# Attention, MLP and mixture of experts on one core: the experts' stage issued in source order, casts placed behind the copies of the products' banks, superblock border and last pair rearranged

## The chip, the cores and the metric

The kernel runs on 1 core of a Trainium2 chip. The metric is the device time of one execution in microseconds (us), smaller is better. Engines are called PE (matrix products), DVE (VectorE), ACT (ScalarE), POOL (GpSimd) and SP (the engine that issues DMAs here).

## The reference

```python
x = attention(q, k, v)                 # linear attention, 2304 tokens x 512
h = x @ moe_w_in; x = max(0.01 * h, h) @ moe_w_out          # 512 -> 2048 -> 512
P = exp(x @ w_gate - max)              # 2304 x 8
for _ in range(8):
    P /= P.sum(1, keepdims=True) + 1e-09; P /= P.sum(0, keepdims=True) + 1e-09; P *= N / E
for e in range(8):
    out += P[:, e:e + 1] * (np.maximum(x @ w1[e], 0.0) @ w2[e])   # 512 -> 1024 -> 512
```

All in fp32. The kernel splits each fp32 matrix into a high part (a cast on ACT) and a low part (a subtraction of that cast, mostly on DVE), and makes three products of them.

## The kernel before, in words

The first quarter computes attention and the MLP. What concerns the change is the experts' stage behind it. It treats the tokens in three superblocks of 768 (`NSB`) and the experts' hidden units in 32 pairs of 128-unit blocks (`NQ`), so there are 96 groups (`NG`), numbered `i`; groups 0 to 31 are superblock 0, 32 to 63 superblock 1, 64 to 95 superblock 2. Each `group(i)` is seven half steps, `t0` to `t6`. In `t0` to `t3` PE makes the seven products of a Strassen-like scheme, six matmuls each, in four PSUM banks (`pa` to `pd`): `pa`, `pb`, `pc`, `pd`, then `pa`, `pc`, `pd` a second time, accumulated on top. Between the two uses of a bank, ACT has to copy its first content out (`c1` from `pa`, the two halves of `c2` from `pc` and `pd`; lines 866, 881, 883). In `t4` to `t6` PE makes the second layer of the pair of groups before: in superblock 0 three token tiles of twelve 512-column matmuls (`y_tile`, tiles `e`), from group 34 on the seven products of `y_pass` (tiles `e` too, 384 columns).

Superblock 0 also prepares the experts' weights. `pair_load` and `second_load` bring the raw pair from DRAM to `mo_t`; POOL makes sums of its quarters (`pair_sums`, `second_sums`); `split` casts on ACT and subtracts on DVE (`pair_w1`, `pair_w2`, `second_split`); `keep` stores the split weights in DRAM (`d`). `second_split` uses three staging buffers in turn (`stage`). Superblocks 1 and 2 read the split weights back through a ring of buffers (`ring_load`). There DVE applies relu and the gate's weight (`relu_p`, into `mo_t`), POOL and DVE subtract (`sub_raw`), and `op_split` casts and subtracts the second layer's operands. In `y_pass`, ACT copies three of the products out (`snap`) and POOL adds them to `c22`; DVE adds the other four (`into`). At a border of superblocks `x_next` makes the split sums of the next 768 tokens. `y_out` transposes a superblock's result on PE, and stores it.

The first stage's order is written by hand (`tc.manual_schedule` for PE, ACT, POOL and SP). `front.close()` ends that before group 0, so in the experts' stage a scheduler orders every engine. The helper that issues all products has one line:

```python
    def split(hi, lo, a):
        nc.scalar.copy(hi, a)
        return lambda: nc.vector.tensor_tensor(lo, a, r32(hi), op=ALU.subtract)
```

The lambda is called in the next half step, by `drain`.

Of the kernel before, what the change touches and what calls it, by code (L numbers as in the profile page):

```python
# [22 lines left out]
def kernel(  # L23
# [163 lines left out]
    def bank(name):  # L187
        pool, tag = spare[0]
        spare.append(spare.pop(0))
        return pool.tile([P, 512], F32, tag=tag, name=name)  # L190

# [192 lines left out]
    def balance():  # L384
        nc.vector.tensor_reduce(mrow, lg, axis=AX.XY, op=ALU.max)
        yield PE_NEXT
        pt = bank("pmx")[:1, :P]
        nc.tensor.transpose(pt, mrow, ident)
        nc.vector.tensor_reduce(mall, pt, axis=AX.X, op=ALU.max, negate=True)
        yield PE_NEXT  # L390
        pt = bank("pmb")[:, :1]
        mm(pt, ones[:1, :], mall, True, True)
        nc.vector.tensor_copy(mneg, pt)
        yield
        nc.scalar.activation(pm, lg, AF.Exp, bias=mneg)
        yield
        for it in range(8):
# [6 lines left out]
            nc.vector.tensor_reduce(cs, pm.rearrange("p t e -> p e t"), axis=AX.X, op=ALU.add)  # L404
            yield PE_NEXT
            pt = bank(f"pcs{it}")[:, :E]
# [7 lines left out]
            yield  # L414
        ready.add("pm")
        yield
        for n, (r0, r1) in enumerate(((0, P), (P, TT * E))):
            yield PE_NEXT
            pt = bank(f"pT{n}")[: r1 - r0, :P]
# [92 lines left out]
    def split(hi, lo, a):  # L512
        nc.scalar.copy(hi, a)  # L513
        return lambda: nc.vector.tensor_tensor(lo, a, r32(hi), op=ALU.subtract)  # L514
# [10 lines left out]
    def pair_w1(i, part):  # L525
# [3 lines left out]
        return split(w1(i)[:, 0, 4:], w1(i)[:, 1, 4:], s_t())  # L529

# [29 lines left out]
    def second_sums(g):  # L560
        a11, a12, a21, a22 = second_quads(g)
        nc.gpsimd.tensor_tensor(a22, a21, a22, op=ALU.add)
        nc.gpsimd.tensor_tensor(a21, a11, a21, op=ALU.subtract)
        nc.gpsimd.tensor_tensor(a11, a22, a11, op=ALU.subtract)
        nc.gpsimd.tensor_tensor(a12, a11, a12, op=ALU.subtract)

    def second_split(g, k):
        a11, a12, a21, a22 = second_quads(g)
        name, a = (("S1", a22), ("S3", a21), ("S2", a11), ("S4", a12))[k]
# [3 lines left out]
        with tc.issue_after(mark[0].ins):  # L573
            f = split(v[:, 0], v[:, 1], a)
# [7 lines left out]
    def x_sums(sb):  # L582

        b = [
# [4 lines left out]
        b11, b12, b21, b22 = b  # L589
        if sb:  # L590
            t1 = hp_.tile([P, KC // 2, BLK], F32, tag="hh", name=f"t1_{sb}")
        else:
            t1 = mo(0, XS // 2).rearrange("p (c n) -> p c n", c=KC // 2)
# [4 lines left out]
        def both(name, a):  # L598
            split(xt(name)[:, 0], xt(name)[:, 1], a)()
            ready.add(("xt", sb, name))  # L600
# [14 lines left out]

    def x_next(sb):
        f = x_sums(sb)
        for i, n in ((0, 2), (2, 4), (4, 5), (6, 8), (5, 6), (8, 9), (9, 11)):
            for g in f[i:n]:
                g()  # L620
            if n in (2, 4, 5, 8):
                yield

    ring = []
    for i in range(NQ, NG + 2):
        if i < NG:
            ring += [d1[i % NQ][WA[n]] for n, _ in FIRST]
        g = i // 2 - 1
        if g >= NQ // 2:
            ring += [d2[g % (NQ // 2)][i % 2, WA[n]] for n, _, _ in SECOND]  # L630
# [26 lines left out]
    def product(o, i, an, bn, start=True):  # L657
# [4 lines left out]
        else:  # L662
            assert FIRST[used[0] % 7 if used[0] < 21 else (used[0] - 21) % 14 - 7][0] == an
# [30 lines left out]
    def relu_split(i, th, u, p):  # L694
        o = hid(i, th)[:, :, u]
        mark[0] = nc.scalar.activation(o[:, 0], p, AF.Relu)
# [37 lines left out]
    def y_pass(g, dt):  # L734
# [7 lines left out]
        bk = {}  # L742
# [10 lines left out]
        def into(a, b):  # L753
            if first_ and a is not c22:
                nc.scalar.copy(a, bk[b])
            else:
                nc.vector.tensor_tensor(a, bk[b], a, op=ALU.add)  # L757

        def step(n):
            an, bn, b = SECOND[n]  # L760
            assert ("op", g, bn) in ready, (g, bn)
            start = b not in bk
# [5 lines left out]
            if bn in ("B11", "T1", "T3"):  # L768
                snap(b)
            else:  # L770
                into({"B21": c11, "B22": dd, "T2": c22, "T4": cc}[bn], b)
            if last and n == 6:
                active.append([y_out(sb, dt, ya), None])

        return step

    def y_out(sb, dt, ya):
# [4 lines left out]
        for th, quads in enumerate(((c11, cc), (dd, c22))):  # L782
            for t in range(TB):
                if t % 2 == 0:
                    yield PE_NEXT
                tt = th * TB + t
                pt = bank(f"po{sb}_{dt}_{tt}")[:, : 2 * P]
# [15 lines left out]
    mark = [None]  # L803

    def group(i):
# [5 lines left out]
        nxt = i + 1 < NQ  # L811
# [6 lines left out]
        if g >= NQ // 2:  # L818
            step = y_pass(g, i % 2)
# [7 lines left out]
        def second_ops(t):  # L827
# [3 lines left out]
            if half == 0 and g >= 0:  # L831
# [5 lines left out]
                if t in (5, 6):  # L837
                    rest.append(second_split(g, t - 5))
            if half == 1:
                if t in (0, 1) and g >= 0:  # L840
                    rest.append(second_split(g, 2 + t))
                if t == 2 and i < NQ:
                    second_load(i - 1)
                    second_load(i)
                if t == 5 and i < NQ:
                    rest.append(pair_w2(i - 1))
                if t == 6 and i < NQ:
                    rest.append(lambda: keep_w2(i - 1))

        def t0():  # L850
            drain((late, rest))
            second_ops(0)
# [6 lines left out]
            if i >= NG:  # L859
                return  # L860
            if i < NQ:
                keep_w1(i)
            if nxt:
                pair_sums(i + 1)
# [3 lines left out]
            add(c1, bk[1], c1)  # L868

        def t1():  # L870
            drain()
            second_ops(1)
# [5 lines left out]
            if i >= NG:  # L878
                return
            product(bk[2], i, "S1", "T1")  # L880
            mark[0] = nc.scalar.copy(c2[:, 1], bk[2])
# [3 lines left out]
            add(c2[:, 1], c2[:, 1], c1)  # L885

        def t2():
            drain()
            second_ops(2)
            if i == NQ + 1:  # L890
                ring_load(18, 22)
            if i >= NG:
                return
# [7 lines left out]
            if i < NQ:  # L901
                pair_load(i + 2)

        def t3():
            if i >= NG:
# [246 lines left out]
```

## Time and profile before

| | us |
|---|---|
| median of 3 runs (lowest, highest) | 2041.34 (2037.67, 2042.96) |
| the profiled execution's own time | 2042.34 |
| its span, first to last instruction | 2040.6 |
| PE busy in the span | 1959.7 (96%) |
| DVE, ACT, POOL busy | 1521.5, 799.2, 678.3 |

The profiled execution stands 1.0 us over the median and 1.7 us over its own span. A busy PE can be a slow PE: its granted clock is a column of the stretches below.

### The profile page before, as it was taken

What the parts mean: (1) busy time and instruction counts of PE and PEld (TensorE: products, weight loads), DVE (VectorE), ACT (ScalarE), POOL (GpSimd) and SP (SyncE); (2) the same over time, 40 slices, a digit from 0 to 9 for tenths busy, and PEclk for the clock granted to TensorE, in tenths of its full rate; (3) what the DMA queues carried; (4) which work ended last, traced back from release to release, by engine and by line L of the source; (5) the groups of instructions that cost most, each with busy time, mean ns of one, the idle gap of its engine ahead of it and who ended that gap; (6) DMA issues with size and microseconds to landing.
All of it is one profiled execution on the core that took longest, in us unless ns stands there. A gap on an engine that the chain in (4) does not pass through costs nothing.

```text
span 2040.6 us, 30223 instructions
## 1 busy us (share of the span) xinstructions
PE 1959.7 (96%) x10757; PEld 1872.9 (92%) x10757; DVE 1521.5 (75%) x2193; ACT 799.2 (39%) x1481; POOL 678.3 (33%) x536
## 2 busy tenths in 40 slices
PE   7999999999998999999999999999989999999998
PEld 6999999999888888888889999999989999999997
DVE  7766535354886778776786888898897888888886
ACT  6744323243543444444333333333343333333332
POOL 4123313111243535343322333334332343343333
PEclk8999999999999999999999999999999999999999
DMA  6402201111678787878768878788777887778784
GB/s 238 165 11 73 62 21 52 42 57 68 216 270 309 257 309 252 307 256 307 259 214 299 252 234 267 254 254 255 253 224 234 257 257 253 253 234 268 252 248 145
DMA packets 237108, 430.44 MB, mean 211 GB/s; under 512 B 19984, under 2 KB 38560, under 8 KB 236960
## 3 DMA queue, kind: packets, MB, share of 16 engines
q1 hardware_dynamic: 236960, 428.51, 63.9%
q8 instruction: 87, 1.43, 0.3%
q14 instruction: 61, 0.50, 0.1%
HBM read 306.20 MB, written 122.23 MB: 210 GB/s over the span
## 4 chain that ended last, share of the span: by engine, by line
PE 40%; DVE 8%; ACT 2%; DMA 1%; issue 1%; POOL 1%; SPq 0%; POOLq 0%; ACTq 0%; DVEq 0%
PE e L193 22%; PE pa L193 5%; PE pc L193 5%; PE pd L193 5%; DVE xs L514 2%; PE pb L193 2%; DVE wa L514 2%; DVE acc L757 2%; DVE mo_t L730 1%; ACT xs L513 1%; DVE c L817 1%; POOL acc L751 1%; ACT c L866 0%; DMA mo_t<-in_w 0%; ACT wa L513 0%
## 5 line engine op out<-in xcount | busy, mean ns | idle before, releaser
L751 POOL TENSOR_TENSOR acc<-acc,acc 128x384 f32<-128x384 f32 x188 | 236.8, 1260 | 406.6 <-ACT acc L750 403.8
L193 PE MATMUL e<-xs,wb_t 128*128 128x384 f32 x1452 | 272.4, 335 | 0.0
L193 PE MATMUL e<-wb_t,xs 128*128 128x512 f32 x1152 | 272.2, 394 | 0.0
L193 PEld LDWEIGHTS e<-wb_t,xs 128*128 128x128 f32 x1152 | 218.4, 190 | 45.2 <-DVE xs L697 0.4
L513 ACT CAST wa<-mo_t 128x768 fp32r<-128x768 f32 (+2 forms) x189 | 159.0, 846 | 242.2 <-DVE mo_t L716 74.9
L193 PEld LDWEIGHTS e<-xs,wb_t 128*128 128x128 f32 x1452 | 253.4, 188 | 0.4
L193 PE MATMUL e<-wa,wb_t 128*128 128x384 f32 x1236 | 235.3, 335 | 5.8 <-DVE acc L757 5.5
L514 DVE TENSOR_TENSOR wa<-mo_t,wa 128x768 fp32r<-128x768 f32 (+2 forms) x189 | 209.9, 1121 | 30.9 <-ACT wa L513 30.5
L193 PEld LDWEIGHTS e<-wa,wb_t 128*128 128x128 f32 x1236 | 216.0, 188 | 7.3 <-DVE acc L757 6.5
L757 DVE TENSOR_TENSOR acc<-e,acc 128x384 f32<-128x384 f32 x244 | 124.1, 546 | 119.2 <-POOL acc L751 118.7
L513 ACT CAST xs<-mo_t 128x768 fp32r<-128x768 f32 x122 | 101.9, 836 | 233.7 <-DVE mo_t L716 93.3
L730 POOL TENSOR_TENSOR mo_t<-mo_t 128x768 f32<-128x768 f32 x64 | 118.5, 1852 | 218.8 <-DVE mo_t L716 211.8
L211 DVE TENSOR_TENSOR hh<-g,hh 128x384 fp32r<-128x384 f32 x96 | 60.5, 630 | 147.8 <-ACT g L210 147.6
L193 PE MATMUL pa<-xs,wb_t 128*128 128x384 f32 x744 | 154.1, 341 | 15.1 <-ACT c L866 13.6
L193 PEld LDWEIGHTS pa<-xs,wb_t 128*128 128x128 f32 x744 | 130.0, 188 | 23.8 <-ACT c L866 23.7
L514 DVE TENSOR_TENSOR xs<-mo_t,xs 128x768 fp32r<-128x768 f32 x122 | 141.6, 1177 | 13.3 <-ACT xs L513 13.3
L193 PE MATMUL pc<-xs,wb_t 128*128 128x384 f32 x744 | 150.7, 337 | 0.0
L193 PE MATMUL pd<-xs,wb_t 128*128 128x384 f32 x744 | 149.7, 335 | 0.0
L716 DVE SCALAR_TENSOR_TENSOR mo_t<-c,mo_t 128x768 f32<-128x768 f32 (+1 forms) x128 | 138.1, 1081 | 3.1
L209 ACT ACTIVATE hh<-ph 128x384 fp32r<-128x384 f32 x96 | 47.3, 493 | 233.1 <-PE y L193 218.3
L520 POOL TENSOR_TENSOR mo_t<-mo_t 128x256 f32<-128x256 f32 x32 | 28.5, 891 | 323.3 <-DMA mo_t<-in_w 190.3
L193 PEld LDWEIGHTS pc<-xs,wb_t 128*128 128x128 f32 x744 | 132.6, 190 | 0.0
(152 smaller groups left out, 3659.2 us busy)
## 6 DMA issues: line engine op xcount, KB each, us to landing
wb_t<-d SPq DMA_DIRECT2D x882, 256.0 KB, 3.2
d<-wa SPq DMA_DIRECT2D x32, 1792.0 KB, 9.1
d<-wb_t SPq DMA_DIRECT2D x90, 512.0 KB, 4.1
mo_t<-in_w SPq DMA_DIRECT2D x64, 512.0 KB, 6.2
raw<-in_wm SPq DMA_DIRECT2D x32, 512.0 KB, 3.7
d<-wa SPq DMA_DIRECT2D x22, 512.0 KB, 3.3
mo_t<-pd SPq DMA_DIRECT2D x32, 192.0 KB, 6.6
v<-in_vt SPq DMA_DIRECT2D x16, 320.0 KB, 5.6
```

The lines of the kernel that those rows point to most:

```text
L193: nc.tensor.matmul(o, a, b, start=start, stop=stop, **more)
L209: nc.scalar.activation(hh[:, 0, :], p, AF.Prelu, alpha=0.01)
L211: nc.vector.tensor_tensor(hh[:, 1, :], g, r32(hh[:, 0, :]), op=ALU.subtract)
L513: nc.scalar.copy(hi, a)
L514: return lambda: nc.vector.tensor_tensor(lo, a, r32(hi), op=ALU.subtract)
L520: nc.gpsimd.tensor_tensor(s[:, 0], a21, a22, op=ALU.add)
L716: nc.vector.scalar_tensor_tensor(o, p, 0.0, r, op0=ALU.max, op1=ALU.mult)
L730: eng.tensor_tensor(raw_q(o), raw_q(x), raw_q(y), op=ALU.subtract)
L751: nc.gpsimd.tensor_tensor(c22, c22, t, op=ALU.add)
L757: nc.vector.tensor_tensor(a, bk[b], a, op=ALU.add)
L817: add = lambda o, x, y: nc.vector.tensor_tensor(o, x, y, op=ALU.add)
```

## The change

Manual order now holds to the end of the program on PE, ACT, POOL and SP: `front.close()` moves behind the last group. DVE's order stays the scheduler's. Inside the groups, `second_ops` and several `op_split` are called behind the products and copies of their half step, and some in another half step; two of the four `second_sums` go from POOL to DVE; the loads of `second_load` go from `t2` to `t0` and `t1`; the casts of the second pair of groups are prepared in the first stage. At the border, sums of the next tokens (`x_ahead`) are made on POOL ahead of time. In `y_pass` the fourth bank is added to `c22` last. The passes of the last two pairs move by a group (`passes`), and the last pass subtracts straight from the banks and stores by column quarter (`y_last`).

```diff
-    def split(hi, lo, a):
+    def split(hi, lo, a, eng=nc.vector):
...
     def second_sums(g):
-        nc.gpsimd.tensor_tensor(a22, a21, a22, op=ALU.add)
+        nc.vector.tensor_tensor(a22, a21, a22, op=ALU.add)
         nc.gpsimd.tensor_tensor(a21, a11, a21, op=ALU.subtract)
-        nc.gpsimd.tensor_tensor(a11, a22, a11, op=ALU.subtract)
+        nc.vector.tensor_tensor(a11, a22, a11, op=ALU.subtract)
...
+    def x_split(sb, name, a):
+        eng = nc.gpsimd if sb > 1 and name in ("B11", "T2") else nc.vector
+        f = split(xt(name)[:, 0], xt(name)[:, 1], a, eng)
...
+    def x_ahead(sb):
...
+        nc.gpsimd.tensor_tensor(t1, b12, b11, op=ALU.subtract)
+        nc.gpsimd.tensor_tensor(t2, b22, t1, op=ALU.subtract)
+        nc.gpsimd.tensor_tensor(b12, b22, b12, op=ALU.subtract)
...
+    def passes(i):
+        if i < NQ + 2 or i == NG - 2:
+            return ()
+        if i < NG - 2:
+            return ((4, i // 2 - 1, i % 2),)
+        return {
+            NG - 1: ((4, LG - 1, 0),),
+            NG: ((0, LG - 1, 1), (4, LG, 0)),
+            NG + 1: ((0, LG, 1),),
+        }[i]
...
     def second_ops(t):
...
-                if t in (5, 6):
-                    rest.append(second_split(g, t - 5))
-            if half == 1:
-                if t in (0, 1) and g >= 0:
-                    rest.append(second_split(g, 2 + t))
-                if t == 2 and i < NQ:
-                    second_load(i - 1)
-                    second_load(i)
-                if t == 5 and i < NQ:
+                if t >= 3:
+                    rest.append(second_split(g, t - 3))
+            if half == 1 and i < NQ:
+                if t < 2:
+                    second_load(i - 1 + t)
+                if t == 6:
                     rest.append(pair_w2(i - 1))
...
         def t0():
-            drain((late, rest))
-            second_ops(0)
+            drain((rest, late))
...
             add(c1, bk[1], c1)
+            second_ops(0)
+            if new and half and i < NG - 1:
+                rest.append(op_split(eg, "T1", raw_q(0)))
...
+    def y_last(n, a, th, h):
+        pt = bank(f"pl{n}")[:, :BLK]
+        for t in range(TB):
+            ts = slice(t * P, (t + 1) * P)
+            nc.tensor.transpose(pt[:, ts], a[:, ts], ident)
...
-    front.close()
     t = END
     for i in range(NG + 2):
...
+    front.close()
```

Three places show how rows move. ACT in superblock 0, from the last casts of group 16 to the copies of group 17; `wa_86` and `wb_t_1584` hold split weights, the `2x4x128` cast is `pair_w2`, the `2x2x128` casts are `second_split`. First before, then now:

```order
L696 ACTIVATE xs_85<-c1_16_6728 128x384
L513 CAST wb_t_1584<-mo_t_3711 128x2x2x128 x3
L866 COPY c1_17_6855<-pa_17_6850 128x384
L513 CAST wb_t_1584<-mo_t_3711 128x2x4x128
L881 COPY c2_17_6854<-pc_17_6852 128x384
L883 COPY c2_17_6854<-pd_17_6853 128x384
```

```order
L526 CAST wa_86<-mo_t_3711 128x2x2x128
L526 CAST wb_t_1584<-mo_t_3711 128x2x2x128
L763 ACTIVATE xs_85<-c2_16_6725 128x768
L977 COPY c1_17_6860<-pa_17_6855 128x384
L1000 COPY c2_17_6859<-pc_17_6857 128x384
L1002 COPY c2_17_6859<-pd_17_6858 128x384
```

The `pair_w2` cast no longer stands between the copies of `pa` and `pc`; its row comes after the group's `pair_w1` casts, near the group's end. The `second_split` casts stand in the even group, ahead of the relu of `c2`.

DVE in superblock 1, from the subtraction of `t3` in group 43 to the first add of group 44; `acc` are the results, `L514`/`L527` the subtractions of splits. First before, then now:

```order
L730 TENSOR_TENSOR mo_t_3711<-mo_t_3711 128x768
L716 SCALAR_TENSOR_TENSOR mo_t_3711<-c1_43_10284,mo_t_3711 128x384
L514 TENSOR_TENSOR wa_86<-mo_t_3711,wa_86 128x768
L514 TENSOR_TENSOR xs_85<-mo_t_3711,xs_85 128x768 x2
L757 TENSOR_TENSOR acc2_81<-e20_1_3_10380,acc2_81 128x384
L757 TENSOR_TENSOR acc2_81<-e20_1_0_10347,acc2_81 128x384
L730 TENSOR_TENSOR mo_t_3711<-mo_t_3711 128x768
L757 TENSOR_TENSOR acc3_82<-e20_1_2_10357,acc3_82 128x384
```

```order
L797 TENSOR_TENSOR mo_t_3711<-mo_t_3711 128x768
L783 SCALAR_TENSOR_TENSOR mo_t_3711<-c1_43_10281,mo_t_3711 128x384
L527 TENSOR_TENSOR xs_85<-mo_t_3711,xs_85 128x768
L527 TENSOR_TENSOR wa_86<-mo_t_3711,wa_86 128x768
L824 TENSOR_TENSOR acc2_81<-e20_1_0_10346,acc2_81 128x384
L797 TENSOR_TENSOR mo_t_3711<-mo_t_3711 128x768
L824 TENSOR_TENSOR acc3_82<-e20_1_2_10356,acc3_82 128x384
```

Ahead of the second subtraction (`mo_t`, the source of the cast that follows) two splits and one add are left of three and two.

DVE at the border, group 63, from the first add of `c1` to the second product's adds; `L596` are the sums of the next tokens. First before, then now:

```order
L817 TENSOR_TENSOR c1_63_13054<-pb_63_13050,c1_63_13054 128x384
L514 TENSOR_TENSOR xs_85<-acc4_83,xs_85 128x768
L596 TENSOR_TENSOR t1_2_13105<-acc5_84,acc4_83 128x768
L596 TENSOR_TENSOR acc5_84<-acc5_84 128x768
L817 TENSOR_TENSOR c2_63_13053<-c2_63_13053 128x384
L716 SCALAR_TENSOR_TENSOR mo_t_3711<-pa_63_13049,mo_t_3711 128x384
```

```order
L921 TENSOR_TENSOR c1_63_13054<-pb_63_13050,c1_63_13054 128x384
L527 TENSOR_TENSOR xs_85<-mo_t_3711,xs_85 128x768
L921 TENSOR_TENSOR c2_63_13053<-c2_63_13053 128x384
L921 TENSOR_TENSOR c2_63_13053<-c2_63_13053,c1_63_13054 128x384
L783 SCALAR_TENSOR_TENSOR mo_t_3711<-pa_63_13049,mo_t_3711 128x384
```

The four sums of the border are gone from DVE; three of them stand on POOL at group 58, one in group 63. DVE has 28 instructions between the first adds of groups 63 and 64 before, 21 now.

## Rows read from the trace of the kernel before

**Rows 1.** The profile's first part: busy us of each engine and instructions.

```profile
PE 1959.7 (96%) x10757; PEld 1872.9 (92%) x10757; DVE 1521.5 (75%) x2193; ACT 799.2 (39%) x1481; POOL 678.3 (33%) x536
```

**Rows 2.** Stretches: length, busy us and instructions by engine, granted clock, DMA share, GB/s.

```profile
395.00:504.33 109.33, 108.02 (x609) 102.85 (x609) 52.30 (x78) 40.10 (x80) 13.82 (x12) 0.98 0.17 58
504.33:638.67 134.34, 131.11 (x667) 116.01 (x666) 108.94 (x196) 61.07 (x102) 46.89 (x45) 1.00 0.71 247
638.67:1041.29 402.62, 371.69 (x1795) 333.12 (x1795) 298.31 (x381) 163.40 (x259) 150.23 (x128) 0.97 0.78 276
1072.31:1505.55 433.24, 426.49 (x2437) 422.20 (x2437) 355.78 (x468) 155.53 (x281) 157.45 (x114) 1.00 0.81 258
1505.55:1580.42 74.87, 66.59 (x361) 64.40 (x361) 64.06 (x87) 31.06 (x57) 23.04 (x16) 0.93 0.73 222
1580.42:1998.96 418.54, 411.66 (x2354) 407.28 (x2353) 346.78 (x454) 149.56 (x269) 153.58 (x111) 1.00 0.81 252
1998.96:2040.57 41.61, 32.49 (x187) 30.36 (x186) 27.80 (x40) 12.37 (x26) 13.38 (x11) 0.97 0.41 125
```

**Rows 3.** The chain that ended last: start, us, engine, tile, line, matmuls.

```profile
1063.20 8.20 PE e L193 x36
...
1078.71 7.28 PE e L193 x42
...
1134.38 1.34 PE pa L193 x6
...
1164.34 1.34 PE pa L193 x6
```

**Rows 4.** Waits of PE in 638.67:1041.29: total us, times, longest.

```profile
PE pc L193 <- ACT c L881: 19.8, 10, 3.6
PE pa L193 <- ACT c L866: 6.6, 2, 5.2
```

**Rows 5.** Timeline, group 17: start, us, engine, instruction, [idle before it <- what ended it].

```profile
782.80 1.42 SPq L510 DMA_DIRECT2D mo_t<-in_w  x1
...
784.91 1.04 ACT L513 CAST wb_t<-mo_t 128x1024 fp32r<-128x1024 f32 x1 [2.90 <-DMA mo_t<-in_w]
...
786.38 1.34 PE L193 MATMUL pc<-xs,wa 128*128 128x384 f32 x6 [2.29 <-ACT c L881]
```

**Rows 6.** Timeline, end of group 43 and start of group 44.

```profile
1212.98 1.84 POOL L730 TENSOR_TENSOR mo_t<-mo_t 128x768 f32<-128x768 f32 x1 [6.63 <-DVE mo_t L716]
1213.22 2.42 DVE L730 TENSOR_TENSOR mo_t<-mo_t 128x768 f32<-128x768 f32 x1
...
1218.54 2.64 DVE L514 TENSOR_TENSOR xs<-mo_t,xs 128x768 fp32r<-128x768 f32 x2
...
1222.04 0.94 DVE L730 TENSOR_TENSOR mo_t<-mo_t 128x768 f32<-128x768 f32 x1
...
1223.01 0.83 ACT L513 CAST wa<-mo_t 128x768 fp32r<-128x768 f32 x1 [4.11 <-DVE mo_t L730]
...
1224.28 1.34 PE L193 MATMUL pa<-xs,wb_t 128*128 128x384 f32 x6 [0.52 <-ACT c L866]
```

**Rows 7.** Timeline at the border and at the end.

```profile
1523.82 1.31 PE L193 MATMUL e<-wa,wb_t 128*128 128x384 f32 x6 [2.94 <-DVE acc L757]
...
2024.57 0.77 PE L789 MATMUL po<-ident,acc 128*128 128x128 f32 x5
...
2031.15 1.20 PE L193 MATMUL e<-wa,wb_t 128*128 128x384 f32 x6
```

**Rows 8.** Groups by line and form in 638.67:1041.29: count, busy us, mean ns, idle before.

```profile
L690 DVE SCALAR_TENSOR_TENSOR acc<-e,pm,acc 128x512 f32<-128x512 f32 x72 | 52.6, 742 | 24.6 <-PE e L193 24.6
...
L565 POOL TENSOR_TENSOR mo_t<-mo_t 128x512 f32<-128x512 f32 x11 | 18.1, 1644 | 0.9
```

**Rows 9.** Waits of ACT in 638.67:1041.29: total us, times, longest.

```profile
ACT wb_t L513 <- DMA d<-wb_t: 33.9, 6, 7.7
```

**Rows 10.** DMA issues in 640:1040: count, KB each, median us to landing.

```profile
d<-wb_t SPq DMA_DIRECT2D x66, 512.0 KB, 4.1
```

More of the change, by code (lines that the diff above doesn't have):

```diff
@@ L598, in both @@
         def both(name, a):
[L599 to L600 removed]
+            x_split(sb, name, a)()
         return (
@@ L802, with ends @@
     rest, late = [], []
-    mark = [None]
+    def ends(i):
+        return NQ < i < NG - 1 and i % NQ == NQ - 1
     def group(i):
@@ L859, in t0 @@
             if i >= NG:
+                y_steps(0)
+                if i == NG:
+                    rest.append(op_split(LG, "T2", raw_q(0)))
+                    rest.append(op_split(LG, "T3", raw_q(1)))
                 return
@@ L878, in t1 @@
             if i >= NG:
+                y_steps(1)
+                if i == NG:
+                    rest.append(op_split(LG, "T4", raw_q(2)))
                 return
             product(bk[2], i, "S1", "T1")
-            mark[0] = nc.scalar.copy(c2[:, 1], bk[2])
+            nc.scalar.copy(c2[:, 1], bk[2])
             product(bk[3], i, "S3", "T3")
@@ L885, in t1 @@
             add(c2[:, 1], c2[:, 1], c1)
+            second_ops(1)
+            if ends(i - 1):
+                rest.append(op_split(eg - 1, "T4", raw_q(2)))
         def t2():
             drain()
-            second_ops(2)
             if i == NQ + 1:
@@ L911, in t3 @@
                 relu_p(i, 1, raw_q(2 * half + 1), c2)
-                if half == 0:
-                    rest.append(op_split(eg, "B11", raw_q(0)))
-                else:
-                    rest.append(op_split(eg, "B21", raw_q(2)))
+                if half:
                     sub_raw(nc.vector, 0, 3, 0)
+                    if not ends(i):
+                        sub_raw(nc.gpsimd, 1, 3, 1)
             else:
@@ L927, in t4, with t5 @@
                 y_tile(pre[0], pre[1])
-            if g >= NQ // 2:
-                for n in range(3):
-                    step(n)
+            y_steps(4)
             drain()
             if nxt:
-                rest.append(pair_w1(i + 1, 1))
+                rest.append(pair_w1(nxt, 1))
             second_ops(4)
+            if new:
+                if half == 0:
+                    rest.append(op_split(eg, "B11", raw_q(0)))
+                else:
+                    rest.append(op_split(eg, "B21", raw_q(2)))
+                    rest.append(op_split(eg, "B22", raw_q(3)))
+        def t5():
+            if pre:
+                y_tile(pre[0], pre[1] + 1)
+            y_steps(5)
+            drain()
+            second_ops(5)
             if new:
@@ L959, in t6 @@
                 y_tile(pre[0], pre[1] + 2)
-            if g >= NQ // 2:
-                for n in range(5, 7):
-                    step(n)
+            y_steps(6)
             drain()
             second_ops(6)
-            if new and half:
-                rest.append(op_split(eg, "T2", raw_q(0)))
+            if new and half and not ends(i) and i < NG - 1:
+                rest.append(op_split(eg, "T3", raw_q(1)))
                 rest.append(op_split(eg, "T4", raw_q(2)))
```

211 lines of the change are left out of this document (147 added, 64 removed).

## Prediction

> **What bounds the kernel now.** I read the busy shares first: PE is busy for 1959.7 us of the span, the next engine, DVE, for 1521.5 [rows 1]. So the end is set by PE, and only PE's pauses and slow stretches can be won. The chain that ended last says what PE's work costs without a pause: a group's seven products, 42 matmuls, take 7.28 us (1.04 each), three token tiles, 36 matmuls, 8.20 us [rows 3]. A bare group is then 15.48 us in superblock 0 and 14.56 us later, where the seven products of `y_pass` stand for the tiles. The order of the built programs has the same 10612 matmuls before and after, so this floor doesn't move.
>
> Next come the stretches, cut where the `pb` product of groups 0, 9, 32, 34, 63, 67 and 95 starts [rows 2]. Against the bare groups:
>
> - Groups 0 to 8 (504.33 on): PE is idle for 134.34 - 131.11 = 3.2 us.
> - Groups 9 to 31: 402.62 - 23 x 15.48 = 46.6 us over. Idle time is 30.9 of it. The rest fits the granted clock: 0.97 on average between 1.0 (2.4 GHz) and 0.5 (1.2 GHz) is 6% of the stretch at the lower level, 24 us, which costs half of that.
> - Superblock 1, groups 34 to 62: 433.24 - 29 x 14.56 = 11.0 us over; superblock 2, groups 67 to 94: 418.54 - 28 x 14.56 = 10.9 us over.
> - The border, groups 63 to 66: 74.87 - 58.24 = 16.6 us, of which 24 transposes take at most 24 x 0.77 / 5 = 3.7 us [rows 7]; 12.9 are left.
> - From group 95 on, 41.61 us: 27 products are 28.1, 24 transposes 3.7, and 8.2 lie between the end of the last product (2031.15 + 1.20) and the span's end [rows 7]; 1.6 are left.
>
> The last view is who ended PE's waits. In superblock 0 they are ends of ACT's copies, ten times that of `pc` [rows 4]. One of them in full, in group 17: the `pair_w2` cast of 1.04 us stands on ACT between the copies of `pa` and `pc`, and waits for a load that SP issued in the same group, at 782.80; it starts at 784.91, the copy follows, and PE has been idle for 2.29 us [rows 5]. In superblock 1 the same happens with `op_split`: a cast of `mo_t` waits for DVE's second subtraction, which ends at 1222.98, ACT's copy of `pa` is behind it, and PE waits 0.52 us [rows 6]; that pair of groups takes 1164.34 - 1134.38 = 29.96 us in place of 29.12 [rows 3].
>
> **The change part by part.** My sum is made against the profiled execution, 2042.3 us, 1.0 over the median.
>
> A, superblock 0. In odd groups the three copies now stand next to each other, the `pair_w2` cast comes some ten us later, and its loads are issued two half steps sooner. In even groups the other `pair_w2` cast is between the copies of `pa` and `pc`, but its data was asked for a group earlier. 1.04 us of cast behind a copy of 0.5 ends before `pc` does, 2.08 us after `pa`. So the 46.6 us go. What is late next: a `second_split` cast that needs its staging buffer back. Only the fourth one does within a group, from the first, whose store lands 4.1 us (median) after its issue [rows 10]; before, such waits took 33.9 / 6 = 5.7 us each [rows 9]. The first cast now comes at `t3`, the fourth at `t6`, some 8 us on, and behind the fourth only the relu of `c2` stands ahead of the next `c1`, which has until that group's fifth product, 4.2 us after its start. I keep 2 us of loss for all pairs, 0 to 16 (1 us each) as bounds.
>
> Moved onto DVE: 32 second sums, two in each pair of groups. DVE has no such row; the lower bound is its 512-column operation of 742 ns, the upper POOL's own 1644 ns [rows 8]. I take the lower, as the operand count is nearest; 1.5 us a pair, at most 3.3. DVE is busy for 298.31 / 11.5 = 25.9 us a pair [rows 2]; with them 27.4 to 29.2 of the 30.96 that PE needs. PE covers it, with four banks and a group between a product and its reuse; without this cover it would be 16 x 1.5 = 24 us.
>
> B, the steady groups of superblocks 1 and 2. Ahead of DVE's second subtraction stand one split and one add fewer: 2.64 / 2 + 0.5 = 1.8 us [rows 6], or 0.5 if the remaining splits each take that split's excess again. Both ends cover the wait of 0.5 us. The 26 pairs with 0.84 us give 21.9; I keep 1 back.
>
> C, the border. Four sums and two subtractions leave DVE for POOL, which is busy 23 us of 75 there [rows 2]; the seven casts are spread over seven half steps. DVE is still the fullest engine of groups 63 and 64, and in group 65 it copies a transposed tile behind a subtraction; PE may wait there as it waited 2.94 us for DVE before [rows 7]. Of 12.9 I keep 4 (0 to 10).
>
> D, the end. The delayed passes fill PE while the last operands are split; 1.0 of 1.6 is won. Behind the last product there are as before a subtraction, transposes, copies, six stores in a row: 8.2 stay.
>
> E, groups 0 to 8. DVE is busy for 108.94 of 134.34 us there already, and gets second sums too, so all 3.2 stay. The preparation of the second pair moves into the first stage (two loads, four sums, two casts, two subtractions), where DVE, ACT and POOL are at most half busy [rows 2]: nothing, or 4 us if PE were to wait for all of it.
>
> Won: A 44.6, B 20.9, C 8.9, D 1.0, together 75.4. 2042.3 - 75.4 = 1966.9, say 1967 us. If all is won, 86.2 give 1956. With the upper bounds of what stays (16, 4, 10 in place of 2, 0, 4) it is 1967 + 24 = 1991.
>
> **The rivals.**
>
> R1, DVE keeps the copies late. In superblock 1 POOL and DVE subtract at the same time: DVE's takes 2.42 us, its twin with POOL idle 0.94 [rows 6], so it ended 0.8 us after POOL's did: about as long as its own work. The new order starts both at `t3` again, and puts POOL's adds of `c22` beside the two splits. If every split is held up, B's 21.9 us stay, and DVE is late in superblock 0 by the 3.3 us a pair of its bound where it is fullest, say half the pairs: 1967 + 21 = 1988 with the first alone, 2010 with both. Against it: 0.5 of 1.8 us suffices. The Trainium skill ("SBUF — State Buffer", section "Who interferes with whom") has DVE instructions with two SBUF inputs and POOL instructions that read SBUF exclude each other for a whole instruction. By that rule the pair of subtractions is this rival's mechanism, and the trace agrees: 2.42 against 0.94.
>
> R2, slower. The fourth `second_split` cast waits for its buffer's store and now stands in fixed order ahead of the next `c1`. For 2048.5 us it must cost 81.5 / 16 = 5.1 us a pair, so the cast must come 5 us beyond its slack, which is 4.2 less the relu and the copy, 2.9: the store would have to land some 12 us after its issue plus what the steps between give. Waits of up to 7.7 us are on record [rows 9], so it isn't excluded; but the first cast has moved ahead by two half steps.
>
> R3, no change: the scheduler before may have hidden with reordering what a fixed order now shows elsewhere, 86 us in many small waits. Nothing in the rows has that size.
>
> **How the numbers follow.** Under 0.3% (6 us) two times of this kernel can't be told apart. The forecast (1953 to 1980) has 0.65, R1 0.23, R2 0.04, R3 0.02, and 0.06 is for less than 1953, through gains in the first groups and behind the last product. Faster 0.94, same 0.02, slower 0.04. The range reaches from 1950 into R1, to 1995; that leaves about 0.15 outside.
>
> **What would show it.** Right: groups of 15.5 us and pairs of 29.1 us in the chain, no PE wait for a copy of `pc`, granted clock 1.0 from group 9 to 31, 1 to 5 us of waits at the border, DVE near 88% of the experts' stage. A is wrong if PE still waits for ACT in superblock 0, most of all at the start of odd groups behind a store; B if pairs stay at 29.9; the whole if DVE has no idle time left while PE waits.

## The result and the profile after

The changed kernel takes 1987.47 us (median of 4 runs, 1986.21 to 1989.11) against 2041.82 before: ratio 0.9738, 95% interval 0.9721 to 0.9755. The forecast was 1967, the range 1950 to 1995. So sign and range held, and 20 us of the forecast gain of 75 did not come. The profiled execution has a span of 1984.4 us.

The stretches that answer to [rows 2], with the same columns, cut where the `pb` product of groups 0, 9, 32, 34, 63, 67 and 94 starts:

```profile
501.34:637.41 136.07, 131.44 (x666) 117.40 (x666) 111.70 (x205) 61.67 (x105) 38.09 (x36) 0.99 0.70 242
637.41:997.75 360.34, 358.67 (x1795) 323.08 (x1795) 292.49 (x394) 160.17 (x256) 144.24 (x114) 1.00 0.86 299
997.75:1041.14 43.39, 34.81 (x157) 30.98 (x157) 32.30 (x42) 13.28 (x21) 6.64 (x4) 0.84 0.74 264
1041.14:1464.24 423.10, 422.53 (x2437) 422.21 (x2437) 347.43 (x473) 159.30 (x280) 186.76 (x117) 1.00 0.82 263
1464.24:1532.94 68.70, 63.36 (x361) 62.28 (x361) 56.94 (x77) 31.04 (x56) 28.80 (x18) 0.98 0.78 243
1532.94:1926.06 393.12, 393.12 (x2270) 393.12 (x2269) 322.57 (x439) 149.81 (x261) 169.42 (x108) 1.00 0.81 261
1926.06:1984.40 58.34, 48.72 (x271) 46.32 (x270) 38.43 (x57) 17.14 (x33) 18.12 (x14) 0.96 0.50 152
```

The steady stretches are clean now: PE is busy without a gap for 393.12 us, which is 27 x 14.56, at clock 1.00. The third line stands out: 8.6 us of idle time in two groups, and a clock of 0.84. Before, these two groups took 31.02 us, without a gap (1041.29 to 1072.31, between two lines of [rows 2]). Beside the prediction's terms (the last stretch of before is 1983.58 to 2040.57; the prediction counted group 94 in B, with 0.8 us of B's gain, and here it lies in the last row):

| stretch | before | after | moved by | forecast |
|---|---|---|---|---|
| up to group 0 | 504.33 | 501.34 | -3.0 | 0 |
| groups 0 to 8 (E) | 134.34 | 136.07 | +1.7 | 0 |
| groups 9 to 31 (A) | 402.62 | 360.34 | -42.3 | -44.6 |
| groups 32, 33 | 31.02 | 43.39 | +12.4 | none made |
| groups 34 to 62, 67 to 93 (B) | 836.40 | 816.22 | -20.2 | -20.9 |
| groups 63 to 66 (C) | 74.87 | 68.70 | -6.2 | -8.9 |
| from group 94 (D) | 56.99 | 58.34 | +1.3 | -1.0 |
| together | | | -56.2 | -75.4 |

What stops PE in group 32, read from the timeline there (start, us, engine, instruction, [idle before <- what ended it]). The SP row at 954.21 is the same pair of loads two groups earlier:

```profile
954.21 2.70 SPq L523 DMA_DIRECT2D mo_t<-in_w  x2
...
987.00 4.53 SPq L706 DMA_DIRECT2D wa<-d  x7
991.57 0.43 SPq L550 DMA_DIRECT2D d<-wa  x1
992.11 0.50 SPq L523 DMA_DIRECT2D mo_t<-in_w  x1
992.65 3.92 SPq L774 DMA_DIRECT2D mo_t<-pd  x2
996.91 1.51 SPq L523 DMA_DIRECT2D mo_t<-in_w  x1
...
1002.81 1.04 ACT L526 CAST wb_t<-mo_t 128x1024 fp32r<-128x1024 f32 x1 [4.91 <-DMA mo_t<-in_w]
...
1004.50 0.46 ACT L977 COPY c<-pa 128x384 f32<-128x384 f32 x1
...
1005.02 2.29 PE L199 MATMUL pa<-xs,wa 128*128 128x384 f32 x6 [3.98 <-ACT c L977]
...
1010.43 1.04 ACT L526 CAST wb_t<-mo_t 128x1024 fp32r<-128x1024 f32 x1 [5.46 <-DMA mo_t<-in_w]
...
1011.90 2.29 PE L199 MATMUL pc<-xs,wa 128*128 128x384 f32 x6 [4.60 <-ACT c L1000]
```

Group 29's loads leave 4.6 us after its `pb` product (949.63). Group 31's (`pb` at 980.85) leave after 11.3 and 16.1 us: SP has seven ring loads (`L706`), the store of the first-layer weights (`L550`) and two loads of the gate's weights (`L774`) ahead of them. They land when the `pair_w2` casts have long been waiting, and ACT's copies of `pa` and `pc` stand behind these casts. The six matmuls behind each wait take 2.29 us, not the 1.34 of [rows 5]: the granted clock was 0.50, its lower level, from 1005.0 to 1014.2, after PE had stood idle for 3.98 us and on through the second pause.

In the kernel before, the scheduler let the two loads leave at 1017.62 and 1019.35, with `pb` at 1018.13. They cost PE a wait there too, one group earlier:

```profile
1017.62 0.52 SPq L510 DMA_DIRECT2D mo_t<-in_w  x1
...
1026.58 1.04 ACT L513 CAST wb_t<-mo_t 128x1024 fp32r<-128x1024 f32 x1 [5.69 <-DMA mo_t<-in_w]
...
1028.06 2.29 PE L193 MATMUL pd<-xs,wa 128*128 128x384 f32 x6 [4.56 <-ACT c L883]
```

Group 31 took 23.16 us for it, and takes 16.90 now. So 6.3 of the 42.3 us won in groups 9 to 31 were won in group 31, and groups 31 to 33 together went from 54.2 to 60.3 us: part of the new loss is this wait, moved and grown.

### The profile page after: what moved, and what is told of

It reads as the page before. It is cut to its first block, busy times and chain, and to the rows that moved or that the text cites. A ratio compares the mean times of both kernels' runs of the same rounds, so it can differ in the third digit from the quotient of the medians.

```text
span 1984.4 us, 30153 instructions
## 1 busy us (share of the span) xinstructions
PE 1938.1 (98%) x10757; PEld 1864.1 (94%) x10757; DVE 1491.1 (75%) x2214; ACT 805.2 (41%) x1480; POOL 708.3 (36%) x514
## 4 chain that ended last, share of the span: by engine, by line
PE 46%; DMA 9%; DVE 6%; POOL 2%; ACT 2%; issue 1%; SPq 1%; DVEq 0%; POOLq 0%; ACTq 0%
PE e L199 23%; PE pc L199 6%; PE pd L199 6%; PE pa L199 6%; DMA mo_t<-in_w 6%; PE pb L199 3%; DMA d<-wb_t 2%; DMA d<-wa 1%; DVE c L921 1%; DVE wa L527 1%; POOL mo_t L534 1%; DVE mo_t L797 1%; DVE mo_t L783 1%; ACT wa L526 1%; DVE wb_t L527 1%
## 5 line engine op out<-in xcount | busy, mean ns | idle before, releaser
L819 POOL TENSOR_TENSOR acc<-acc,acc 128x384 f32<-128x384 f32 x188 | 277.0, 1473 | 301.7 <-ACT acc L818 292.0
L199 PE MATMUL e<-xs,wb_t 128*128 128x384 f32 x1392 | 262.7, 335 | 5.6 <-DVE acc L824 3.0
L199 PEld LDWEIGHTS e<-xs,wb_t 128*128 128x128 f32 x1392 | 242.8, 188 | 6.8 <-DVE acc L824 3.7
L199 PE MATMUL e<-wa,wb_t 128*128 128x384 f32 x1296 | 244.3, 336 | 0.4 <-DVE acc L824 0.3
L527 DVE TENSOR_TENSOR wa<-mo_t,wa 128x768 fp32r<-128x768 f32 (+2 forms) x194 | 201.3, 1053 | 36.9 <-ACT wa L526 35.7
L199 PEld LDWEIGHTS e<-wa,wb_t 128*128 128x128 f32 x1296 | 227.5, 189 | 1.0 <-DVE acc L824 0.7
L818 ACT COPY acc<-e 128x384 f32<-128x384 f32 x188 | 90.3, 480 | 292.5 <-PE e L199 277.8
L527 DVE TENSOR_TENSOR xs<-mo_t,xs 128x768 fp32r<-128x768 f32 x119 | 125.6, 1066 | 37.1 <-ACT xs L526 37.1
L199 PEld LDWEIGHTS pd<-xs,wb_t 128*128 128x128 f32 x744 | 130.9, 188 | 3.2 <-DVE xs L527 3.1
L783 DVE SCALAR_TENSOR_TENSOR mo_t<-c,mo_t 128x768 f32<-128x768 f32 (+1 forms) x128 | 128.9, 1011 | 3.0
```

The costliest lines, as they stand in the source:

```text
L199: nc.tensor.matmul(o, a, b, start=start, stop=stop, **more)
L527: return lambda: eng.tensor_tensor(lo, a, r32(hi), op=ALU.subtract)
L783: nc.vector.scalar_tensor_tensor(o, p, 0.0, r, op0=ALU.max, op1=ALU.mult)
L818: nc.scalar.copy(t, bk[b])
L819: nc.gpsimd.tensor_tensor(c22, c22, t, op=ALU.add)
```

## The experiments

Ratios are to the kernel before on the same chip; the changed kernel has 0.9738 (0.9721 to 0.9755). Stretches come from the traces, cut as above.

| run | median us | ratio (95%) | groups 0-8 | 9-31 | 32, 33 | 34-62 | 63-66 | from 94 |
|---|---|---|---|---|---|---|---|---|
| before | 2041.82 | 1 | 134.3 | 402.6 | 31.0 | 433.2 | 74.9 | 57.0 |
| changed | 1987.47 | 0.9738 | 136.1 | 360.3 | 43.4 | 423.1 | 68.7 | 58.3 |
| scheduler, new source | 1978.78 | 0.9696 (0.9681, 0.9710) | 130.9 | 356.9 | 31.0 | 426.6 | 72.6 | 58.6 |
| fixed, old source | 2078.56 | 1.0187 (1.0171, 1.0202) | 148.5 | 375.5 | 41.3 | 446.5 | 83.7 | 61.9 |
| scheduler up to 33, then fixed | 1965.25 | 0.9643 (0.9629, 0.9658) | 130.9 | 356.9 | 31.0 | 423.1 | 70.2 | 56.3 |

### Loads ahead of the ring loads

```diff
         def t0():
...
-            if i == NQ - 1:
-                ring_load(0, 7)
...
             second_ops(0)
+            if i == NQ - 1:
+                ring_load(0, 7)
...
         def t1():
...
-            if i == NQ - 1:
-                p_load(1, 0)
...
             second_ops(1)
+            if i == NQ - 1:
+                p_load(1, 0)
```

> The changed kernel with one thing moved on SP: in group 31 the raw loads of pairs 30 and 31 are issued ahead of the seven ring loads and of the two gate loads, not behind them. Theory (the loads come late because of what SP issues ahead of them): in group 32 both casts on ACT wait less than 1.5 us each, PE's waits of 3.98 and 4.60 us there and the slow clock behind them go, group 32 takes 15.5 to 17 us in place of 27.9, and the time falls by 11 to 12 us, to about 1975.5 us. Rival (the transfers themselves are slow in this stretch, or the buffers are not free sooner): at least 6 of the 12.4 us stay, time 1981 to 1987. Second rival (the ring loads are now late): PE waits 3 us or more for them at the start of group 32, time about 1979.

1983.11 us, ratio 0.9718 (0.9704 to 0.9733). The time lies where the first rival had it, the stretch fits neither: groups 32 and 33 took 35.74 us, 7.7 less, and group 31 1.8 more. SP and ACT in its timeline say why:

```profile
988.79 1.36 SPq L523 DMA_DIRECT2D mo_t<-in_w  x1
990.25 7.40 SPq L706 DMA_DIRECT2D wa<-d  x7
...
998.59 0.38 SPq L523 DMA_DIRECT2D mo_t<-in_w  x1
998.69 1.04 ACT L526 CAST wb_t<-mo_t 128x1024 fp32r<-128x1024 f32 x1
...
1005.22 1.04 ACT L526 CAST wb_t<-mo_t 128x1024 fp32r<-128x1024 f32 x1 [4.02 <-DMA mo_t<-in_w]
```

The first load is ahead of the ring loads and its cast no longer waits. The second is issued a half step later and so still behind them, and its cast waits 4.02 us. The edit did only half of what its expectation said.

### The first ring loads in group 30

Two runs, in both of which `p_load(1, 0)` goes from `t1` of group 31 to behind `ring_load(7, 14)` in `t4`. The first:

```diff
         def t5():
...
             second_ops(5)
+            if i == NQ - 2:
+                rest.append(lambda: ring_load(0, 7))
```

The second:

```diff
         def t5():
...
             y_steps(5)
+            if i == NQ - 2:
+                ring_load(0, 7)
             drain()
```

> The changed kernel, fixed order throughout; the first seven ring loads are issued at the end of group 30 in place of the start of group 31, and the two gate loads of group 31 three half steps later, so that nothing of these stands ahead of the raw loads of pairs 30 and 31 on SP. Theory (SP's burst at group 31's start makes both loads late, also by sharing the transfer engines with them): both loads are issued within 8 us of the pb product of group 31, groups 32 and 33 take 31 to 35 us in place of 43.4, time 1976 to 1980. Rival (the transfer engines are full in this stretch whatever the order on SP): what is won there comes back as waits for ring loads, time 1982 to 1987.

> The changed kernel, fixed order throughout; the first seven ring loads are issued in group 30 ahead of the last two stores of its second-half splits, the gate loads of group 31 behind the next ring loads. Theory (the raw loads of pairs 30 and 31 are late by what stands ahead of them on SP, and by the share of the transfers that the burst takes): both loads are issued 7 us or less after the pb product of group 31, groups 32 and 33 take 31 to 34 us in place of 43.4, time 1975 to 1979. Rival (the transfers of this stretch fill all engines in any such order): 37 us or more, time 1981 to 1985.

The first: 1983.77 us, ratio 0.9734 (0.9719 to 0.9748). Its ring loads still left only at 988.61, behind two stores, the raw loads at 993.54, 10.2 us after `pb`, and groups 32 and 33 took 38.1 us. The second: 1980.12 us, ratio 0.9710 (0.9694 to 0.9726). SP's timeline:

```profile
979.13 3.97 SPq L706 DMA_DIRECT2D wa<-d  x7
...
990.30 2.67 SPq L523 DMA_DIRECT2D mo_t<-in_w  x2
```

With nothing but four stores between them and the ring loads, both loads leave 7.0 us after `pb` (983.33), the casts don't wait, groups 32 and 33 take 33.1 us, at a clock of 1.00, and 10.3 of the 12.4 us are back. So in the trace the cause is the burst of ring loads and gate loads ahead of the raw loads; whether by SP's time or by the transfers that it puts ahead of them, the run does not part. The time came out 1 us above the theory's range and moved by less than the intervals can part, since the other stretches together were 3.9 us longer in this execution.

### Fixed order and source apart

The new source with the scheduler:

```diff
+    front.close()
     t = END
     for i in range(NG + 2):
...
-    front.close()
     assert not active and not plan and not rest and not late, (active, plan)
```

> The changed kernel, but the fixed order ends ahead of group 0 again, so the scheduler orders every engine in the experts' stage from the new source. Theory (the casts stay behind the copies only because the order is fixed): waits of PE for ACT's copies come back in superblock 0, at least half of the 42 us won there, time 2008 to 2030. Rival (the new places in the source suffice): within 6 us of the changed kernel, 1981 to 1993.

The old source in fixed order:

```diff
-    front.close()
     t = END
     for i in range(NG + 2):
...
+    front.close()
     assert not active and not plan and not rest and not late, (active, plan)
```

> The kernel before with one line moved: the fixed order holds to the end, the source is the old one. Theory (the gain needs the new places; the old source in fixed order puts the casts ahead of the copies too): pairs of superblocks 1 and 2 stay at 29.9 us or more, and superblock 0 keeps waits of PE for ACT; time 2025 or more, it can be well above the kernel before. Rival (order alone is the gain): within 10 us of the changed kernel.

I expected the first to lose half of A; it beats the changed kernel. With the scheduler and the new source, superblock 0 is clean (356.9 us for groups 9 to 31, 31.0 for 32 and 33, 5.2 less in groups 0 to 8), and groups 34 to 62 and 67 to 93 take 3.5 and 3.3 us more. The old source in fixed order is slower than the kernel before, as expected: it wins 27 us in groups 9 to 31, and loses 14 in groups 0 to 8, 10 in 32 and 33, and more behind them. In groups 9 to 30 it takes 347.9 us, against 379.5 before and 343.4 in the changed kernel: there the fixed order alone wins most of A, more than its expectation had. In group 31 it loses 4.4 us, and there seven ring loads again stand ahead of the raw loads on SP (1004.77 and 1015.99), a cast waits 14.18 us for one of them, and PE 11.9 us. So the new source clears A wholly without the fixed order, and the fixed order clears most of it without the new source; on top of the new source it costs in superblock 0 and pays a little behind it. In the steady groups of superblocks 1 and 2 the old source in fixed order is slower than before (pairs of 30.9 us), so the gain there is the new source's. That gave the next version.

```diff
+    front.close()
     t = END
     for i in range(NG + 2):
+        if i == NQ + 2:
+            front.enter_context(tc.manual_schedule(engines={E_.PE, E_.Activation, E_.Pool, E_.SP}))
```

> The changed kernel, with groups 0 to 33 in the scheduler's order and the fixed order from group 34 on. Theory (the fixed order loses in superblock 0, in its first groups and at the border behind group 31, and wins in the steady groups of superblocks 1 and 2): the stretches of the run with the scheduler up to group 34 (520.4 us) and those of the changed kernel from there (943.3) add up to a span of 1963.7 us, time 1964 to 1969. Rival (the stretches do not add, since the ring loads and operands that the fixed part finds stand otherwise): waits of more than 5 us in groups 34 to 36, time 1972 or more.

1965.25 us: the stretches add. Its stretches of groups 9 to 31, and 32 and 33:

```profile
631.68:988.53 356.85, 356.85 (x1796) 323.39 (x1796) 292.32 (x393) 161.82 (x254) 123.20 (x109) 1.00 0.86 303
988.53:1019.55 31.02, 31.02 (x158) 28.10 (x157) 26.09 (x37) 10.18 (x17) 7.00 (x4) 1.00 0.60 210
```

PE has no gap from group 9 to 33. That its time is near the 1967 forecast for the changed kernel is in part chance: 3.4 us against the kernel before come from groups 0 to 8, where the forecast had nothing.

### The loads of superblock 0

```diff
-                if t < 2:
-                    second_load(i - 1 + t)
+                if t == 2:
+                    second_load(i - 1)
+                    second_load(i)
...
             add(c2[:, 0], bk[2], c1)
+            second_ops(2)
```

> The changed kernel, with both second-half raw loads of an odd group issued in its third half step again, casts at their new places. Theory (the casts need the earlier loads: a load lands 9.7 us after its issue, and the first cast comes some 13 us after the group's pb product): both casts wait 2 to 4 us, PE waits 1 us or more in each of 15 pairs, superblock 0 takes 15 to 50 us more. Rival (the new places of the casts alone won it): within 3 us of the changed kernel.

1990.58 us, ratio 0.9768 (0.9753 to 0.9783); groups 9 to 31 took 360.1 us as in the changed kernel. The rival holds in the stretch (the time lies 3.1 us off), and SP tells why: in group 17 both loads left from 767.52 on, 4.4 us after `pb`, and in the changed kernel from 766.56 on, also 4.4. The calls stand up to two half steps later, the place in SP's queue hardly moves, since three stores that wait for DVE, 9.4 us together, stand ahead either way. The test of late loads is therefore group 32, not this run.

### The steady groups

Two partial undoings: the old half steps of B21, T2, T3 and POOL's subtraction; and the add to `c22` at once. The first:

```diff
         def t3():
...
                 if half:
+                    rest.append(op_split(eg, "B21", raw_q(2)))
                     sub_raw(nc.vector, 0, 3, 0)
-                    if not ends(i):
-                        sub_raw(nc.gpsimd, 1, 3, 1)
...
         def t4():
...
-                    rest.append(op_split(eg, "B21", raw_q(2)))
                     rest.append(op_split(eg, "B22", raw_q(3)))
+                    if not ends(i):
+                        sub_raw(nc.gpsimd, 1, 3, 1)
...
         def t5():
...
                         sub_raw(nc.vector, 2, 0, 2)
-                    if i < NG - 1:
-                        rest.append(op_split(eg, "T2", raw_q(0)))
+                        if i < NG - 1:
+                            rest.append(op_split(eg, "T3", raw_q(1)))
...
         def t6():
...
-                rest.append(op_split(eg, "T3", raw_q(1)))
+                rest.append(op_split(eg, "T2", raw_q(0)))
                 rest.append(op_split(eg, "T4", raw_q(2)))
+            elif new and half and i < NG - 1:
+                rest.append(op_split(eg, "T2", raw_q(0)))
```

> The changed kernel, with the operand splits of odd groups in superblocks 1 and 2 at their old half steps (the cast of T1 stays where it is): B21 in t3, B22 and POOL's subtraction in t4, DVE's second subtraction and T3 in t5, T2 and T4 in t6, order still fixed. Theory (what stands ahead of DVE's second subtraction makes the cast of T4, and with it the copy of pa, late): the pairs go back toward 29.9 us, 26 times 0.4 to 0.9 us, time 1998 to 2011. Rival (the fixed order or the later add to c22 suffices): pairs stay at 29.12, time within 3 us of the changed kernel.

The second:

```diff
-            elif bn == "T2":
-                later_c22.append(b)
             else:
-                x = into({"B21": c11, "B22": dd, "T4": cc}[bn], b)
-                if n == (4 if final else 6):
-                    with tc.issue_after(x.ins):
-                        into(c22, later_c22.pop())
+                into({"B21": c11, "B22": dd, "T2": c22, "T4": cc}[bn], b)
```

> The changed kernel with the bank of T2 added to c22 as soon as it is done, not last in its pass. Theory (the pairs of superblocks 1 and 2 are won by the places of the operand splits, not by the later add): pairs stay at 29.12 us, time 1985 to 1991. Rival (the add stands on DVE behind POOL's adds to the same tile, and what waits behind it makes the splits late): pairs of 29.5 us or more, time 1995 or more.

The first: 2038.43 us, ratio 0.9988 (0.9978 to 0.9998), pairs of 31.0 us, worse than the 29.97 of the kernel before and more than twice the loss that the theory had. The direction was right, the mechanism another: the cast of T3 on ACT now waits for POOL's subtraction, which stands behind POOL's adds to `c22`, and in fixed order the copy of `pa` stands behind that cast.

```profile
1191.37 4.80 POOL L819 TENSOR_TENSOR acc<-acc,acc 128x384 f32<-128x384 f32 x3 [10.41 <-ACT acc L818]
...
1196.13 1.84 POOL L797 TENSOR_TENSOR mo_t<-mo_t 128x768 f32<-128x768 f32 x1
...
1198.00 0.84 ACT L526 CAST xs<-mo_t 128x768 fp32r<-128x768 f32 x1 [5.21 <-POOL mo_t L797]
...
1200.73 1.32 PE L199 MATMUL pa<-xs,wb_t 128*128 128x384 f32 x6 [1.59 <-ACT c L977]
```

The second: 2006.96 us, ratio 0.9842 (0.9827 to 0.9857), pairs of 29.53 us, and 5 us more in group 58. Here my theory fell and the rival held. DVE's add to `c22` waits 2.00 us for POOL's three adds (1184.11 to 1188.23), everything behind it on DVE is late, the subtraction ahead of T4's cast too:

```profile
1188.27 0.56 DVE L824 TENSOR_TENSOR acc<-e,acc 128x384 f32<-128x384 f32 x1 [2.00 <-POOL acc L819]
...
1191.92 0.83 ACT L526 CAST wa<-mo_t 128x768 fp32r<-128x768 f32 x1 [2.59 <-DVE mo_t L797]
```

### The sums on DVE, the end, the border

```diff
-        nc.vector.tensor_tensor(a22, a21, a22, op=ALU.add)
+        nc.gpsimd.tensor_tensor(a22, a21, a22, op=ALU.add)
...
-        nc.vector.tensor_tensor(a11, a22, a11, op=ALU.subtract)
+        nc.gpsimd.tensor_tensor(a11, a22, a11, op=ALU.subtract)
```

> The changed kernel with all four second sums of a pair of groups on POOL again. Theory (the two sums on DVE, 1.4 us a pair, are covered, and so would be POOL's): superblock 0 within 3 us of the changed kernel, time 1985 to 1991. Rival (POOL's sums, one behind the other, make the casts and stores of the second splits late, and the loads behind them): superblock 0 takes 5 us more or worse, time 1992 or more.

1985.36 us, ratio 0.9739 (0.9720 to 0.9757): no difference in time. In the trace groups 9 to 31 took 357.4 us, 3.0 less: in the fixed order the sums on DVE are not quite free, while with the scheduler the stretch is clean with them. DVE is none the less busier in that stretch without its two sums, 295.9 us for 372 instructions against 292.5 for 394: POOL's own busy time rose from 144.2 to 179.1 us beside it.

The old end; the operand splits of the last pair also go back to the places of the other pairs:

```diff
     def passes(i):
-        if i < NQ + 2 or i == NG - 2:
+        if i < NQ + 2:
             return ()
-        if i < NG - 2:
-            return ((4, i // 2 - 1, i % 2),)
...
+        return ((4, i // 2 - 1, i % 2),)
...
-        final = g == LG and dt == 1
+        final = False
```

> The changed kernel with the end as before: one pass in each of the last groups, six stores of token tiles at the end, no stores by column quarter. Theory (the moved passes lost 2.2 us against the kernel before from group 94 on, since DVE is full when they start): the stretch from the pb product of group 94 on goes from 58.3 to 56.2 us or less, time 1985. Rival (old passes cost more in fixed order, the operands of the last pair come too late for them): 60 us or more, time 1989 or more.

1994.58 us, ratio 0.9784 (0.9768 to 0.9800); from group 94 on 65.3 us, so the rival holds. In fixed order the old end costs 7.0 us more than the new one.

The border, on the version with the scheduler up to group 33:

```diff
         rest.append(x_split(sb, "T1", t1))
+        if sb > 1:
+            rest.append(x_split(sb, "T3", b12))
...
-        rest.append(x_split(sb, "T3", b12))
+        if sb == 1:
+            rest.append(x_split(sb, "T3", b12))
...
-                if t % 2:
+                if t % 2 and sb == NSB - 1:
                     nc.vector.tensor_copy(o, pt)
```

> The kernel with groups 0 to 33 in the scheduler's order (1965.25 us), and two edits at the border behind group 63: the cast and subtraction of the next tokens' T3 two half steps sooner, and all copies of transposed tiles on ACT there. Theory (PE's waits of 2.81, 2.24 and 0.51 us there are the late split of T3 and DVE's copies of tiles): these go, groups 63 to 66 take 64 to 66 us in place of 70.2, time 1959 to 1962. Rival (DVE is full in this stretch, so the waits only change their place): at least 4 of the 5.6 us stay, time 1964 or more.

1965.16 us, ratio 0.9640 (0.9620 to 0.9661), no difference from 0.9643. Groups 63 to 66 took 69.2 us, 1.0 less, which is not clear of noise: in the fixed-order runs that leave this stretch as it is, it took 68.7 to 70.3 us. PE's waits at the border, of the version without this edit and then of this one, fit the rival: the wait gets shorter at T3's split and ends for DVE's copies of tiles, and others come up in its place (two more of 0.4 and 0.3 us stand behind the three shown).

```profile
PE pd L199 <- DVE xs L527: 2.8, 1, 2.8
PE e L199 <- DVE acc L895: 2.2, 1, 2.2
PE e L199 <- ACT acc L897: 0.5, 1, 0.5
```

```profile
PE pd L199 <- DVE xs L527: 1.8, 1, 1.8
PE pa L199 <- ACT c L977: 0.9, 1, 0.9
PE e L199 <- ACT acc L897: 0.6, 1, 0.6
```

## Why the prediction was right, and where it failed

**The step that failed** is in A: "its loads are issued two half steps sooner", with the stretches cut so that groups 32 and 33, which had no loss before, were in none. I followed the loads by their calls and not by their place in SP's queue, which a fixed order makes binding. Between the calls of group 31 SP also has ring loads and gate loads. There the loads leave 11 and 16 us after `pb`; 12.4 of the 19.2 us between forecast and trace lie there, and the early ring loads gave 10.3 back. That the time still lies in the range is partly luck: the range reached to 1995 for R1, and the loss came in a stretch that the sum had left out.

The step was wrong in the steady groups too, and did no harm there. In group 17 the loads left at 779.16 and 782.80 before, with `pb` at 779.77; now they leave from 766.56 on, with `pb` at 762.17, so against `pb` they leave 3 to 5 us later, not sooner. (The cast at 784.91 of [rows 5] had waited for the load of 779.16, which landed 5.7 us later, and not for the one of 782.80, which took 10.0 us.) The cast still waits 3.96 us for its load, but it stands near the end of the group, ahead of no copy that PE waits for:

```profile
766.56 2.61 SPq L523 DMA_DIRECT2D mo_t<-in_w  x2
...
776.92 1.05 ACT L526 CAST wb_t<-mo_t 128x1024 fp32r<-128x1024 f32 x1 [3.96 <-DMA mo_t<-in_w]
```

**A** otherwise held: 42.3 of 44.6 in groups 9 to 31, and PE waits there for no copy of ACT any more. Its only waits there are four for DVE's subtraction of the weights, 1.7 us together, 1.1 of it in group 31. The fourth `second_split` cast, on which R2 hung, cost nothing that PE saw. The explanation by the cast's place holds for the changed kernel, but it is not the only way: in the run with the scheduler the same source comes out with the loads early and the cast ahead of the copy of `pa` (group 17, `pb` at 756.57), and PE does not wait either.

```profile
750.92 0.42 SPq L523 DMA_DIRECT2D mo_t<-in_w  x1
...
756.15 1.05 ACT L526 CAST wb_t<-mo_t 128x1024 fp32r<-128x1024 f32 x1 [4.53 <-DMA mo_t<-in_w]
757.10 0.47 ACT L977 COPY c<-pa 128x384 f32<-128x384 f32 x1
```

The cast's place alone, with all else as before, was not tried. The sums on DVE were sized too small, 1.5 us a pair for 1.11 and 0.69, within the bounds; but DVE's busy time did not grow to 27.4 us a pair, it is 292.49 / 11.5 = 25.4. So of the signs that I had named the one on DVE did not come: it is busy for 81% of the experts' stage, not 88%.

**B** held in size, 20.2 of 20.9. The cast of T4 now ends its wait early enough; the timeline of the end of group 43 and the start of 44 (`pb` at 1186.74), against [rows 6]:

```profile
1187.16 0.94 DVE L797 TENSOR_TENSOR mo_t<-mo_t 128x768 f32<-128x768 f32 x1
...
1188.14 0.84 ACT L526 CAST wa<-mo_t 128x768 fp32r<-128x768 f32 x1 [1.85 <-DVE mo_t L797]
1188.88 0.47 ACT L977 COPY c<-pa 128x384 f32<-128x384 f32 x1
```

The copy ends 2.6 us after `pb` starts; before it ended 3.8 us after (1224.28 against 1220.47). These 1.2 us lie between the 0.5 and the 1.8 that I had. What I counted was right, but not all that matters: the run with the early add to `c22` puts one add more ahead, and that add's wait for POOL's adds gives 0.4 us a pair back.

**C** was mis-sized: 6.2 in place of 8.9, within its bounds of 0 to 10. The waits are where I put them, a late split in group 64 and DVE's copy in group 65. **D** came out 1.3 us the wrong way; the same code took 56.3 us in the mixed version, at a clock of 0.98 against 0.96 here, and 56.6 to 58.8 in other runs that leave it as it is, so its sign is not settled. What holds it back is DVE again, whose subtractions run beside POOL's adds, and PE waits 2.99 us:

```profile
1946.06 5.06 POOL L819 TENSOR_TENSOR acc<-acc,acc 128x384 f32<-128x384 f32 x3
...
1946.84 3.43 DVE L527 TENSOR_TENSOR xs<-mo_t,xs 128x768 fp32r<-128x768 f32 x2
...
1950.79 1.34 PE L199 MATMUL e<-xs,wb_t 128*128 128x384 f32 x6 [2.99 <-DVE acc L824]
```

**R1** gave 1988, close to the time that came, but that is chance: its reason was that B's 21.9 us stay, and 20.2 of them were won. (Its second figure, 2010, adds 22 us where 3.3 us in half of 16 pairs are 26.) Its mechanism is there at single places, the one above and group 31, where two subtractions of DVE take 4.48 us while POOL makes the sums of the next tokens; the line's least duration, for the smaller of the two, is 0.68:

```profile
980.17 4.48 DVE L527 TENSOR_TENSOR wa<-mo_t,wa 128x768 fp32r<-128x768 f32 x2
```

```profile
981.55 2.55 POOL L652 TENSOR_TENSOR acc<-acc 128x768 f32<-128x768 f32 x1
```

```profile
L527 DVE TENSOR_TENSOR wa<-mo_t,wa x60: 679/949/2315, 637.1 to 982.3; 128x768 fp32r<-128x768 f32 x23, 128x1024 fp32r<-128x1024 f32 x22, 128x512 fp32r<-128x512 f32 x15
```

The stores that wait for these subtractions stand ahead of the ring loads, so this is part of the same delay. How much of it was not tried apart. The rule in the Trainium skill ("SBUF — State Buffer", section "Who interferes with whom"), by which such instructions of the two engines shut each other out for a whole instruction, fits these rows.

**E** was wrong by small amounts of both signs. Groups 0 to 8 lost 1.7 us, and with the scheduler they are 5.2 us shorter than in the changed kernel, so the fixed order costs there; most of it lies in group 2 (21.3 us in place of 17.8), where PE waits 3.1 us for a cast. No run undid that place by itself. That the time up to group 0 fell by 3.0 us is not clear of noise: the runs that differ from the changed kernel only behind it took 501.3 to 504.0 us.

## What to carry to other kernels

When a scheduler's order is made a fixed one, read each in-order queue, the DMA issuer's first, at every place where two phases meet: a load counts from the instruction ahead of it there, not from the line that calls it. Cut the sum's stretches without leaving any out, those without a loss before most of all. And change order and placement apart: here either of the two cleared most of the first superblock's waits, the new source was the gain behind it, and the fixed order on top of it paid in one phase and cost in another, so that each phase with its better order gave 1965 us.

## What was not expected of the hardware

A raw load of 512 KB needs 9.7 us from issue to landing (median, from 640 to 965 us) in the changed kernel and 5.5 in the one with the scheduler:

```profile
mo_t<-in_w SPq DMA_DIRECT2D x43, 512.0 KB, 9.7
```

```profile
mo_t<-in_w SPq DMA_DIRECT2D x39, 512.0 KB, 5.5
```

Each row takes two kinds of raw load together. For the loads of `second_load` (`L523`) alone the medians are 9.8 and 5.3 us, for those of `pair_load` (`L519`) 9.6 and 7.9, though the DMA share of groups 9 to 31 is 0.86 in both runs. The scheduler lets the two loads of `second_load` leave 3.3 us apart in group 17, the fixed order 1.3 us apart; whether that is the cause no run tests.
